# Attention scores in four row tiles, PSUM banks in rotating pairs, output products in column tiles

## The chip, the cores and the metric

One NeuronCore of one Trainium2 chip runs the whole program in one launch. The metric is the device time in microseconds, the median of several executions; lower is better. One further execution was taken with the hardware profiler.

## The reference

Two mixers work on 2048 tokens of 448 features and are blended by a gate for each token. Cut to what matters:

```python
def _A_ref(x, wq, wk, wv, wo):            # 16 heads of 28, one key and one value head
    q = (x @ wq).reshape(B, S, H, Dh).transpose(0, 2, 1, 3)
    k, v = x @ wk, x @ wv
    scores = einsum("bhqd,bkd->bhqk", q, k) * Dh ** -0.5
    o = einsum("bhqk,bkd->bhqd", softmax(scores), v)
    return o.transpose(0, 2, 1, 3).reshape(B, S, H * Dh) @ wo

def _B_ref(x, w1, w2, w3, w4):
    h = gelu(layernorm(x) @ w1)           # four groups of channels, shifted by +1, -1, +2, -2 tokens
    x1 = x + shifted(h) @ w2
    return x1 + gelu(layernorm(x1) @ w3) @ w4

g = sigmoid((x * gate_w).sum(-1))
out = g * _A_ref(...) + (1 - g) * _B_ref(...)
```

All of it is float32. Queries and keys are large here (`A_wq` and `A_wk` are scaled by over 40), so the scores need more than one rounded product: the kernel splits an operand into a rounded high part (type `F32R`) and the rest, and sums three products: high by high, high by low, low by high.

## The kernel before

The order of the instructions of every engine is the order in which the kernel writes them (`manual_schedule`). Waits come from a tracker of tiles: who writes a tile waits for the earlier readers of it. The kernel has three stages.

*Projections and token mixing.* `stage_q` makes queries, keys, values and gate sums from split products (`proj`: eleven matmuls of 512 columns into one PSUM bank); `q_out` copies them out with ScalarE (L297) and sends them to DRAM (`qd`). `stage_w1` and `stage_w2` do the first half of the second mixer. Products rotate over four banks (`mm1`: two of `mm_tile`, two of their own). `stage_kv` and `split_k` fetch the keys back and set them as three bands of 32 partitions (high, high, low) in `kS`.

*MLP.* For each of four blocks of 512 tokens and 14 chunks `f` of the hidden layer, `w3_part` makes a chunk with `proj` into one of two `mm_tile` banks, ScalarE takes two GELUs from the bank (L668, L669), VectorE makes the low part, and `w4_part` adds twelve products of 448 columns to four accumulators, two chunks behind. The last chunk of the last block is left for the next stage (`w4_job`).

*Attention.* A unit is four heads by 512 queries; there are 16 units of 16 key tiles (128 keys). For each key tile and head one matmul of 98 rows (three bands of 28 used rows and, in rows 96 and 97, the negated score maximum in two parts) gives the scores in a bank of its own (L901), and ScalarE takes the exponential into a tile `p` (L903). Seven banks rotate, and an eighth holds `pv`. Every few key tiles a visit (`VISITS`) does the products with the values (`pv_group`, L870): for each key tile four matmuls into the four column tiles of 32 of the array, side by side, in plain float32; they add up over the whole unit in `pv`. In between stand, at places written out by hand, estimates of the next unit's maxima (`max_part`, L210 and L211, over the first 32 keys), the products of the unit before with the output weights (`wo_job`, L812 to L816, three split products for each 128 tokens), the products left from the MLP (L841 to L845), and the splitting of the queries of a later unit (`q_begin`). At a unit's end VectorE copies `pv` out (L778); the sums of the exponentials go through memory (`sums_begin`, `recip`) and come back as factors for `norm` (L796).

After the last unit a tail transposes the last result, divides, does its output products and looks whether any sum overflowed; only then a slow second pass would run.

Of the kernel before, what the change touches and what calls it, by code (L numbers as in the profile page):

```python
# [31 lines left out]
PB = 22  # L32
# [9 lines left out]
def gated_mix_kernel(  # L42
# [25 lines left out]
    identR = keep.tile([P, P], F32R, name="identR")  # L68
    nc.vector.tensor_copy(identR, ident)
    x1 = keep.tile([P, NT, D], F32, name="x1")  # L70
    kS = keep.tile([P, S], F32R, name="kS")
# [14 lines left out]
    nc.gpsimd.memset(f32(kS)[96:128, :], 1.0)  # L86

    def mm_tile(name):
        return psA.tile([P, 512], F32, tag="mm", bufs=2, name=name)

    def misc_tile(name):
        return psA.tile([P, 512], F32, tag="misc", bufs=1, name=name)
# [86 lines left out]
    qs_of = [None, None]  # L179

    def q_load(u, raw):
        b, g = divmod(u, NG)
        qr_of[u] = raw
        nc.sync.dma_start(raw[0:4 * DH], qd[g, 0:4 * DH, 512 * b:512 * b + 512])

    def q_split(u, qh, ql):
        qr = qr_of.pop(u)[0:4 * DH]
        qh_of[u], ql_of[u] = qh[0:4 * DH], ql[0:4 * DH]
        nc.vector.tensor_copy(qh_of[u], qr)
        nc.vector.tensor_sub(ql_of[u], qr, f32(qh_of[u]))  # L190

    def q_rows(u):
        q_of[u] = qs_of[u % 2]
        for r, part in enumerate((qh_of[u], ql_of[u], qh_of[u])):
            nc.sync.dma_start(f32(q_of[u])[32 * r:32 * r + DH], f32(part))

    NU = NB * NG
    q_of = {}
    qr_of, qh_of, ql_of = {}, {}, {}
    mx_of = {}  # L200
    mc_of = {}

    def max_tile(name):
        return psA.tile([P, 512], F32, tag="mx", bufs=1, name=name)

    def max_part(u, t, tile_of):
        if t == 0:
            mx_of[u] = late.tile([P, 4, 4], F32, tag="mr", bufs=2, name=f"mr_{u}")
        ps = tile_of(f"m_{u}_{t}")[:, 0:4 * MK].rearrange("p (j k) -> p j k", j=4)
        nc.tensor.matmul(ps, qh_of[u][:, t * P:(t + 1) * P], khd[0:4 * DH], start=True, stop=True)  # L210
        nc.vector.reduce_max(mx_of[u][:, :, t], ps, axis=AX.X)  # L211

    def max_full(u, tile_of):
        mr = late.tile([P, 4, 4], F32, tag="mr", bufs=2, name=f"mf_{u}")
        for j in range(4):
            for t in range(4):
                mk = late.tile([P, NB], F32, tag="mk", bufs=2, name=f"mk_{u}_{j}_{t}")
                for kb in range(NB):
                    ps = tile_of(f"mf_{u}_{j}_{t}_{kb}")
                    nc.tensor.matmul(ps, q_of[u][0:96, j, t * P:(t + 1) * P], kS[0:96, kb * 512:kb * 512 + 512],  # L220
                                     start=True, stop=True)
                    nc.vector.reduce_max(mk[:, kb:kb + 1], ps, axis=AX.X)
                nc.vector.reduce_max(mr[:, j, t:t + 1], mk, axis=AX.X)
        mx_of[u] = mr

    def max_end(u):
# [7 lines left out]
        for p in range(4):  # L234
            nc.sync.dma_start(f32(qs_of[u % 2])[96:98, :, :].rearrange("k j (t p q) -> k p (j t) q", p=4, q=32)[:, p],
                              mrow[32 * p:32 * p + 32, :])
# [4 lines left out]
    with tc.tile_pool(name="s1b", bufs=1) as s1b, \  # L241
# [80 lines left out]
        kf_of = {}  # L322

        def stage_kv(b):
            cols = slice(512 * b, 512 * b + 512)
            kf = s1b.tile([96, 512], F32, tag="kf", bufs=2, name=f"kf_{b}")
            for r in range(3):
                for g in range(2):
                    nc.sync.dma_start(kf[32 * r + 16 * g:32 * r + 16 * g + 16, :], qd[g, 4 * DH:P, cols])
            for g in range(2):  # L330
                nc.sync.dma_start(vT[32 * b + 16 * g:32 * b + 16 * g + 16, :], qd[2 + g, 4 * DH:P, cols])
            kf_of[b] = kf

        def split_k(b):
            cols = slice(512 * b, 512 * b + 512)
            kf = kf_of[b]
            nc.gpsimd.tensor_copy(kS[0:96, cols], kf)
            nc.gpsimd.tensor_tensor(kS[64:96, cols], kf[64:96, :], f32(kS)[64:96, cols], ALU.subtract)
# [207 lines left out]
        split_k(0)  # L546
# [14 lines left out]
        split_k(1)  # L561
# [3 lines left out]
        split_k(2)  # L565
# [4 lines left out]
        khd = late.tile([P, 4, MK], F32R, name="khd")  # L570
        qh0 = late.tile([P, 512], F32R, tag="qh0", bufs=1, name="qh0")
        qs_of[0] = late.tile([P, 4, 512], F32R, name="qs0")
# [8 lines left out]
        def load_w34(i, pool):  # L581
            w3h.append(pool.tile([P, 4, 2 * P], F32R, name=f"w3h_{i}"))
            w3l.append(pool.tile([P, 4, 2 * P], F32R, name=f"w3l_{i}"))
            last = late if 2 * i + 2 == NF else pool
            w4h.append(last.tile([P, 2, D], F32R, name=f"w4h_{i}"))
            w4l.append(last.tile([P, 2, D], F32R, name=f"w4l_{i}"))
# [46 lines left out]
        split_k(3)  # L633
# [10 lines left out]
    with tc.tile_pool(name="s2", bufs=1, reuse_waits="tile") as s2, \  # L644
# [5 lines left out]
        fills = [lambda t=t: max_part(0, t, max_tile if t % 2 else misc_tile) for t in range(4)]  # L650
# [6 lines left out]
        def w3_part(b, f):  # L657
# [3 lines left out]
            if (b, f) == (NB - 1, NF - 1):  # L661
                gh = late.tile([P, 512], F32R, tag="qh0", bufs=1, name="gh_late")
                gl = late.tile([P, 512], F32R, name="gl_late")
            else:
                gh = s2.tile([P, 512], F32R, tag="gh", bufs=3, name=f"gh_{b}_{f}")
                gl = s2.tile([P, 512], F32R, tag="gl", bufs=3, name=f"gl_{b}_{f}")
            gf = s2.tile([P, 512], F32, tag="gf", bufs=2, name=f"gf_{b}_{f}")
# [14 lines left out]
        for b in range(NB):  # L682
            acc = [ps2.tile([P, 512], F32, tag="acc", bufs=4, name=f"acc_{b}_{t}") for t in range(4)]
            gs = {}
            for f in range(NF):
# [24 lines left out]
                if b == 1 and f == 1:  # L710
                    for z in (khd, qs_of[0][0:96]):
                        nc.gpsimd.memset(f32(z), 0.0)
                    for j in range(4):
                        nc.sync.dma_start(f32(khd)[j:4 * DH:4, j, :], f32(kS)[0:DH, 0:MK])
                    q_load(0, s2a.tile([P, 512], F32, tag="xn", bufs=1, name="qr_0"))
                if b == 1 and f == 5:
                    q_split(0, qh0, s2.tile([P, 512], F32R, tag="gl", bufs=3, name="ql_0"))
                    q_rows(0)
# [9 lines left out]
            if b == NB - 1:  # L728
                last_g = gs[NF - 1]
# [9 lines left out]
    with tc.tile_pool(name="s3", bufs=1, reuse_waits="tile") as s3, \  # L739
            tc.tile_pool(name="ps3", bufs=1, space=PSUM, reuse_waits="tile") as ps3:  # L740
        woh = s3.tile([P, 4, D], F32R, name="woh")
        wol = s3.tile([P, 4, D], F32R, name="wol")

        banks = [mm_tile("bank_0"), mm_tile("bank_1"), misc_tile("bank_2")]
        banks += [ps3.tile([P, 512], F32, name=f"bank_{i}") for i in range(3, 7)]

        def bank(name):
            ps = banks.pop(0)
            banks.append(ps)
            return ps  # L750

        qs_of[1] = s3.tile([P, 4, 512], F32R, name="qs1")
        nc.gpsimd.memset(f32(qs_of[1])[0:96], 0.0)
        def q_fetch(u):
            if u < NU:
                q_load(u, s3.tile([P, 512], F32, tag="qr", bufs=1, name=f"qr_{u}"))

        def q_begin(u):
            q_split(u, s3.tile([P, 512], F32R, tag="qh", bufs=2, name=f"qh_{u}"),
                    s3.tile([P, 512], F32R, tag="ql", bufs=1, name=f"ql_{u}"))  # L760
# [3 lines left out]
        q_rows(1)  # L764
# [11 lines left out]
        def sums_begin(u, pv):  # L776
            o = s3.tile([P, 512], F32, tag="o", bufs=2, name=f"o_{u}")
            nc.vector.tensor_copy(o, pv)  # L778
# [15 lines left out]
        def norm(u, o, rb):  # L794
            on = s3.tile([P, 512], F32, tag="onf", bufs=2, name=f"on_{u}")
            nc.vector.tensor_mul(on, o, rb)  # L796
            onh = s3.tile([P, 512], F32R, tag="onh", bufs=2, name=f"onh_{u}")
            onl = s3.tile([P, 512], F32R, tag="onl", bufs=2, name=f"onl_{u}")
            nc.gpsimd.tensor_copy(onh, on)  # L799
            nc.gpsimd.tensor_tensor(onl, on, f32(onh), ALU.subtract)  # L800
            on_of[u] = (onh, onl)
# [3 lines left out]
        def wo_job(u, t, end=None):  # L805
            b, g = divmod(u, NG)
            n = 4 * b + t
            tok = slice(t * P, (t + 1) * P)
            onh, onl = on_of[u]
            held = banks.pop(0)  # L810
            ps = held[:, 0:D]
            nc.tensor.matmul(ps, onh[:, tok], woh[:, g, :], start=True, stop=False)  # L812
            yield
            nc.tensor.matmul(ps, onh[:, tok], wol[:, g, :], start=False, stop=False)  # L814
            yield
            nc.tensor.matmul(ps, onl[:, tok], woh[:, g, :], start=False, stop=True)  # L816
            banks.append(held)
# [10 lines left out]
        woraw = s3.tile([P, 4, D], F32, name="woraw")  # L828
        nc.sync.dma_start(woraw, wo.rearrange("(g p) n -> p g n", p=P))
        nc.gpsimd.tensor_copy(woh, woraw)  # L830
        nc.gpsimd.tensor_tensor(wol, woraw, f32(woh), ALU.subtract)

        weigh_x1(NT - 4, NT)

        def w4_job(t):
            n = NT - 4 + t
            tok = slice(t * P, (t + 1) * P)
            gh, gl = last_g
            held = banks.pop(0)
            ps = held[:, 0:D]  # L840
            nc.tensor.matmul(ps, gh[:, tok], w4h[-1][:, 1, :], start=True, stop=False)  # L841
            yield
            nc.tensor.matmul(ps, gh[:, tok], w4l[-1][:, 1, :], start=False, stop=False)
# [249 lines left out]
```

## Time and profile before

| | |
|---|---|
| Median of 3 runs | 957.46 us (957.17 to 958.8) |
| Profiled execution, span from first to last instruction | 957.7 us; nothing is given of it beside the span |
| TensorE busy | 948.7 us, 99% |
| ScalarE busy | 648.2 us, 68% of the span; 94 us of each 100 in the attention stage |
| VectorE, GpSimd busy | 278.7 us, 115.9 us |
| First score product (L901), last value product (L870) | at 401.04 us; ends at 944.85 us |
| Granted TensorE clock | 0.998 on the mean |

PE is TensorE's matmuls, PEld its weight loads, DVE VectorE, ACT ScalarE, POOL GpSimd, SP SyncE. Times are in us, but the mean of one instruction in a group is in ns. A row of the timeline has the start, the length until the last of the merged instructions ends, the engine, the line, the operation, what it writes and reads, and how many; in brackets the idle time of the engine before it and what ended it. A row of a group has, after the bar, the time in which at least one of them ran, the mean of one, and the idle time before them. A row of the windows has the stretch, its length, the busy time of PE, PEld, DVE, ACT and POOL with the number of instructions, the granted clock, and the share and rate of the DMA engines. Matmuls overlap: a matmul's length holds the time that it needs to get through the array, so the distance from one start to the next is what a stream of them costs.

### The profile page before, as it was taken

How to read it: one execution, taken by the hardware profiler on the slowest of the kernel's cores; microseconds unless marked ns; L12 is line 12 of the kernel's file. 1: busy time of each engine (PE TensorE's matmuls, PEld its weight loads, DVE VectorE, ACT ScalarE, POOL GpSimd, SP SyncE). 2: the span in 40 equal slices, each digit the busy share in tenths (PEclk: the TensorE clock that was granted, in tenths of full speed). 3: DMA queues.
4: the chain of work that ended last, by engine and by line, in shares of the span. 5: the costliest groups of instructions: out<-in, count | busy, mean ns of one | idle time of the engine just before them, and what ended most of it. 6: DMA issues, size and time to landing. Idle time of an engine off the chain costs nothing.

```text
span 957.7 us, 13557 instructions
## 1 busy us (share of the span) xinstructions
PE 948.7 (99%) x5187; PEld 631.2 (66%) x5187; DVE 278.7 (29%) x573; ACT 648.2 (68%) x1266; POOL 115.9 (12%) x139
## 2 busy tenths in 40 slices
PE   9999999999999999999999999999999999999996
PEld 6788888888888888755555555455555555545544
DVE  4664364532423411221222112122121222212112
ACT  5532444332222222499999999999999999999994
POOL 3344300200001410040000000000000000000000
PEclk9999999999999999999999999999999999999999
DMA  9823552201300300111011021011111101210101
GB/s 312 274 70 76 144 165 83 80 14 29 83 1 1 83 1 10 28 54 48 21 42 42 22 79 52 27 26 51 52 51 40 51 13 40 80 51 9 35 13 42
DMA packets 45319, 57.33 MB, mean 60 GB/s; under 512 B 9856, under 2 KB 28096, under 8 KB 45248
## 3 DMA queue, kind: packets, MB, share of 16 engines
q1 hardware_dynamic: 42224, 50.93, 18.4%
q10 hardware_dynamic: 3024, 5.47, 1.5%
q8 instruction: 42, 0.69, 0.3%
q14 instruction: 29, 0.24, 0.1%
HBM read 32.19 MB, written 11.67 MB: 46 GB/s over the span
## 4 chain that ended last, share of the span: by engine, by line
PE 98%; DMA 1%; DVE 0%; ACT 0%; issue 0%; SPq 0%; ACTq 0%
PE bank L901 28%; PE pv L870 25%; PE acc L678 5%; PE acc L680 5%; PE acc L679 5%; PE g L134 4%; PE g L135 4%; PE g L136 4%; PE bank L816 1%; PE bank L814 1%; PE bank L812 1%; PE g L137 1%; PE g L138 1%; PE h L134 1%; PE h L135 1%; PE h L136 1%
## 5 line engine op out<-in xcount | busy, mean ns | idle before, releaser
L903 ACT ACTIVATE p<-bank 128x512 f32<-128x512 f32 x1024 | 511.4, 639 | 33.1 <-PE bank L901 30.7
L901 PE MATMUL bank<-qs,kS 98*128 98x512 f32 x1024 | 305.8, 410 | 0.0
L901 PEld LDWEIGHTS bank<-qs,kS 98*128 98x128 f32 x1024 | 184.1, 189 | 134.3 <-issue 93.1
L870 PE MATMUL pv<-p,vext 128*32 128x512 f32 x2048 | 243.1, 598 | 0.0
L668 ACT ACTIVATE gh<-g 128x512 fp32r<-128x512 f32 x55 | 32.9, 598 | 183.6 <-PE g L138 183.6
L870 PEld LDWEIGHTS pv<-p,vext 128*32 128x32 f32 x2048 | 58.9, 109 | 114.9 <-issue 108.0
L670 DVE TENSOR_TENSOR gl<-gf,gh 128x512 fp32r<-128x512 f32 x55 | 38.2, 695 | 163.6 <-ACT gf L669 159.3
L678 PE MATMUL acc<-w4h,gh 128*128 128x448 f32 x220 | 80.2, 365 | 0.0
L680 PE MATMUL acc<-w4h,gl 128*128 128x448 f32 x220 | 80.0, 364 | 0.0
L679 PE MATMUL acc<-w4l,gh 128*128 128x448 f32 x220 | 79.8, 363 | 0.0
L824 DVE SCALAR_TENSOR_TENSOR ot<-bank,gg,ot 128x448 f32<-128x448 f32 x44 | 30.0, 684 | 146.9 <-ACT p L903 95.1
L799 POOL CAST onh<-on 128x512 fp32r<-128x512 f32 x15 | 9.2, 611 | 471.8 <-DVE on L796 471.8
L134 PE MATMUL g<-ah,w3h 128*128 128x512 f32 x168 | 65.8, 392 | 0.0
L135 PE MATMUL g<-al,w3h 128*128 128x512 f32 x168 | 65.7, 391 | 0.0
L136 PE MATMUL g<-ah,w3l 128*128 128x512 f32 x168 | 65.7, 391 | 0.0
L211 DVE TENSOR_REDUCE mr<-bank 128x4 f32<-128x128 f32 x60 | 17.6, 293 | 108.5 <-PE bank L210 108.5
L678 PEld LDWEIGHTS acc<-w4h,gh 128*128 128x128 f32 x220 | 41.3, 188 | 4.2
L679 PEld LDWEIGHTS acc<-w4l,gh 128*128 128x128 f32 x220 | 41.3, 188 | 4.2
L680 PEld LDWEIGHTS acc<-w4h,gl 128*128 128x128 f32 x220 | 41.3, 188 | 3.1
L778 DVE COPY o<-pv 128x512 f32<-128x512 f32 x15 | 10.4, 692 | 99.4 <-PE pv L870 99.4
L136 PEld LDWEIGHTS g<-ah,w3l 128*128 128x128 f32 x168 | 31.5, 188 | 7.0
L135 PEld LDWEIGHTS g<-al,w3h 128*128 128x128 f32 x168 | 31.5, 188 | 5.7
(196 smaller groups left out, 965.5 us busy)
## 6 DMA issues: line engine op xcount, KB each, us to landing
qs<-qh SPq DMA_DIRECT2D x32, 224.0 KB
qd<-qf ACTq DMA_DIRECT2D x16, 256.0 KB
rb<-rd SPq DMA_DIRECT2D x15, 256.0 KB
x<-in_x_dram SPq DMA_DIRECT2D x4, 896.0 KB
xd<-xt SPq DMA_DIRECT2D x16, 224.0 KB
w34raw<-in_w_dram SPq DMA_DIRECT2D x7, 512.0 KB
qr<-qd SPq DMA_DIRECT2D x16, 224.0 KB
qs<-ql SPq DMA_DIRECT2D x16, 224.0 KB
```

Source lines behind the costliest of these rows:

```text
L134: nc.tensor.matmul(ps, wh[:, c, :], ah[:, c, :], start=(c == 0), stop=False)
L135: nc.tensor.matmul(ps, wh[:, c, :], al[:, c, :], start=False, stop=False)
L136: nc.tensor.matmul(ps, wl[:, c, :], ah[:, c, :], start=False, stop=False)
L668: nc.scalar.activation(gh, ps, AF.Gelu_apprx_tanh)
L670: nc.vector.tensor_sub(gl, gf, f32(gh))
L678: nc.tensor.matmul(ps, gh[:, tok], w4h[i][:, k, :], start=(f == 0), stop=False)
L679: nc.tensor.matmul(ps, gh[:, tok], w4l[i][:, k, :], start=False, stop=False)
L680: nc.tensor.matmul(ps, gl[:, tok], w4h[i][:, k, :], start=False, stop=(f == stop))
L824: nc.vector.scalar_tensor_tensor(ot_of[n], ps, gg[:, n:n + 1], before, op0=ALU.mult, op1=ALU.add)
L870: nc.tensor.matmul(pv[32 * j:32 * j + 32, :], vext[:, kt, :], ps[j], start=(kt == 0), stop=(kt == NT - 1), tile_position=(0, 32 * j))
L901: nc.tensor.matmul(ps, kS[0:98, kt * P:(kt + 1) * P], q_of[u][0:98, j, :], start=True, stop=True)
L903: nc.scalar.activation(p, ps, AF.Exp, scale=SCALE)
```

## The change

- Keys and queries stand in four bands of 32 partitions, one for each head: the keys four times (`kh` high, `kl` low), the queries one head a band (`qh`, `ql`), with the negated maxima in two more rows of a band. A key tile's scores are three rounds (high by high, high by low, low by high) of four matmuls, each 32 rows tall, in four row tiles of the array and into four PSUM banks.
- PSUM is four tiles of two banks. In the attention stage the pairs rotate: two for each key tile, and after every two key tiles a spare one, whose first half takes the value products of the two key tiles before, and whose second half takes a job. The earlier stages use two of these pairs: `mm_tile` gives the halves of `two_mm` in turn, `misc_tile` and `max_tile` the halves of `two_mx`.
- A step of the main loop is two key tiles. The first one's exponentials are two of 512 columns and one of 1024. Of the second one, VectorE copies the first pair to SBUF and ScalarE takes the exponential there in place; the second pair goes as before, 1024 at once. Thus five exponentials in a step instead of eight.
- The value products no longer add up over a unit in PSUM: each step's two key tiles are summed there, and VectorE adds them to `o` in SBUF (`values_end`).
- Output products, and those left from the MLP, are plain float32 in four column tiles of 32 tokens (`by_columns`); the splits of their operands are gone.
- The maxima of a unit are four matmuls into one bank with one reduction. `gf` has one buffer instead of two. `split_k` comes later, for all blocks together.

The core of the diff:

```diff
-PB = 22
+PB = 6
...
+    two_mm = psA.tile([P, 2, 512], F32, name="two_mm")
+    two_mx = psA.tile([P, 2, 512], F32, name="two_mx")
...
     def mm_tile(name):
-        return psA.tile([P, 512], F32, tag="mm", bufs=2, name=name)
+        mm_turn[0] += 1
+        return two_mm[:, (mm_turn[0] + 1) % 2]
...
+    def scores(u, kt, ps):
+        kh = kh_of[0]
+        keys = slice(kt * P, (kt + 1) * P)
+        for r, (k, q) in enumerate(((kh, qh_of[u]), (kh, ql_of[u]), (kl, qh_of[u]))):
+            for j in range(4):
+                h = slice(32 * j, 32 * j + 32)
+                nc.tensor.matmul(ps[j], k[h, keys], q[h, :], start=(r == 0), stop=(r == 2), tile_position=(32 * j, 0))
...
+        def values_end(u, pv):
+            if u not in o_of:
+                o_of[u] = s3.tile([P, 512], F32, tag="o", bufs=2, name=f"o_{u}")
+                nc.vector.tensor_copy(o_of[u], pv)
+            else:
+                nc.vector.tensor_add(o_of[u], o_of[u], pv)
...
+        def by_columns(ps, a, t, w):
+            for i in range(4):
+                c = t * P + 32 * i
+                nc.tensor.matmul(ps[32 * i:32 * i + 32, :], a[:, c:c + 32], w, start=True, stop=True,
+                                 tile_position=(0, 32 * i))
...
+        for c in range(NU * NT // 2 + 1):
+            u, i = divmod(c, NT // 2)
+            k = 2 * c
+            if u < NU:
+                ps, p = score_tiles(u, 2 * i, "p")
+                exps(p, slice(0, 1), ps[0][:, 0:1])
+                exps(p, slice(1, 2), ps[0][:, 1:2])
+                exps(p, high, ps[1])
+                p_of[k] = p
+                ps, p = score_tiles(u, 2 * i + 1, "p")
+                nc.vector.tensor_copy(p[:, low], ps[0])
+                exps(p, high, ps[1])
+                exps(p, low)
+                p_of[k + 1] = p
+            spare = pair()
+            if c:
+                v = divmod(c - 1, NT // 2)[0]
+                pv = spare[:, 0]
+                values(k - 2, pv, True, False)
+                values(k - 1, pv, False, True)
+                if (v, i) != (NU - 1, 0):
+                    values_end(v, pv)
...
+            if i == 3 and u + 1 < NU:
+                max_part(u + 1, range(4), spare[:, 1])
+                max_end(u + 1)
+            elif i > 3 and jobs:
+                jobs.pop(0)(spare[:, 1])
```

Here `score_tiles` takes two pairs and calls `scores`, `exps` is one ScalarE instruction over the named heads, and `values` is the four matmuls of one key tile with the values, as before.

More of the change, by code (lines that the diff above doesn't have):

```diff
@@ L794, in norm, with wo_job @@
         def norm(u, o, rb):
[L795 to L801, printed above, removed]
+            on_of[u] = s3.tile([P, 512], F32, tag="on", bufs=2, name=f"on_{u}")
+            nc.vector.tensor_mul(on_of[u], o, rb)
+        def by_columns(ps, a, t, w):
[3 more added lines that the diff above has]
+                                 tile_position=(0, 32 * i))
         ot_of = {}
-        def wo_job(u, t, end=None):
+        def wo_job(u, t, bank, end=None):
             b, g = divmod(u, NG)
             n = 4 * b + t
[L808 to L817, printed above, removed]
+            ps = bank[:, 0:D]
+            by_columns(ps, on_of[u], t, wof[:, g, :])
             before = x1[:, n, :] if g == 0 else ot_of[n]
@@ L826, in wo_job, with w4_job @@
                 nc.sync.dma_start(out[0, n * P:(n + 1) * P, :], ot_of[n])
[L828 to L831, printed above, removed]
         weigh_x1(NT - 4, NT)
-        def w4_job(t):
+        def w4_job(t, bank):
             n = NT - 4 + t
[L837 to L843, printed above, removed]
-            yield
-            nc.tensor.matmul(ps, gl[:, tok], w4h[-1][:, 1, :], start=False, stop=True)
-            banks.append(held)
-            nc.vector.scalar_tensor_tensor(x1[:, n, :], ps, gi[:, n:n + 1], x1[:, n, :], op0=ALU.mult, op1=ALU.add)
@@ L864, in pv_group, with exps, score_tiles, values @@
+        p_of = {}
+        def exps(p, heads, source=None):
+            nc.scalar.activation(p[:, heads], p[:, heads] if source is None else source, AF.Exp, scale=SCALE)
+        def score_tiles(u, kt, name):
+            ps = [pair(), pair()]
+            scores(u, kt, [ps[j // 2][:, j % 2] for j in range(4)])
+            return ps, s3.tile([P, 4, 512], F32, tag="p", bufs=PB, name=f"{name}_{u}_{kt}")
+        def values(k, pv, first, last):
             u, kt = divmod(k, NT)
-            if kt == 0:
-                pv_of[u] = max_tile(f"pv_{u}")
@@ L924, in gated_mix_kernel @@
-        assert not sums and not norms
-        u = NU - 1
-        pv = pv_of.pop(u)
-        o = s3.tile([P, 512], F32, tag="o", bufs=2, name=f"o_{u}")
-        onh = s3.tile([P, 512], F32R, tag="onh", bufs=2, name=f"onh_{u}")
-        onl = s3.tile([P, 512], F32R, tag="onl", bufs=2, name=f"onl_{u}")
-        on_of[u] = (onh, onl)
+                nc.tensor.matmul(pv[32 * j:32 * j + 32, :], vext[:, kt, :], p[:, j],
+                                 start=first, stop=last, tile_position=(0, 32 * j))
@@ L932, in gated_mix_kernel, with bank @@
+        assert not sums and not norms and not jobs
+        u = NU - 1
+        banks = [q[:, h] for q in pairs for h in range(2)]
+        def bank(name):
+            ps = banks.pop(0)
+            banks.append(ps)
+            return ps
+        part = o_of.pop(u)
+        o = s3.tile([P, 512], F32, tag="o", bufs=2, name=f"oo_{u}")
+        on = s3.tile([P, 512], F32, tag="on", bufs=2, name=f"on_{u}")
+        on_of[u] = on
         toks = [slice(t * P, (t + 1) * P) for t in range(4)]
@@ L969, in tail_wo @@
         def tail_wo(t):
[L970 to L971 removed]
+            wo_job(u, t, bank(f"wo_{t}"), end)
         def keep_warm(n):
```

291 lines of the change are left out of this document (117 added, 174 removed).

## The prediction

> **What bounds the kernel now.** First the head of the page and its chain of work:
>
> ```profile
> span 957.7 us, 13557 instructions
> PE 948.7 (99%) x5187; PEld 631.2 (66%) x5187; DVE 278.7 (29%) x573; ACT 648.2 (68%) x1266; POOL 115.9 (12%) x139
> PE 98%; DMA 1%; DVE 0%; ACT 0%; issue 0%; SPq 0%; ACTq 0%
> PE bank L901 28%; PE pv L870 25%; PE acc L678 5%; PE acc L680 5%; PE acc L679 5%; PE g L134 4%; PE g L135 4%; PE g L136 4%; PE bank L816 1%; PE bank L814 1%; PE bank L812 1%; PE g L137 1%; PE g L138 1%; PE h L134 1%; PE h L135 1%; PE h L136 1%
> ```
>
> TensorE is the chain, and the scores (L901) with the products with the values (L870) are over half of it. The span stands 0.2 us above the median of the runs, so both serve. Next the attention stage by windows, and its groups:
>
> ```profile
> 500.00:600.00 100.00, 100.00 (x612) 53.39 (x608) 21.27 (x51) 94.05 (x189) 5.66 (x6) 1.00 0.16 47
> L903 ACT ACTIVATE p<-bank 128x512 f32<-128x512 f32 x1024 | 511.4, 639 | 33.1 <-PE bank L901 30.7
> ```
>
> ScalarE is busy 94 us in 100 and TensorE all of them: two engines near their limits, covered by seven PSUM banks in rotation. The period of a unit (four heads, 512 queries) is read off the copies of `pv`, 14 units apart, in the timeline:
>
> ```profile
> 436.85 0.69 DVE L778 COPY o<-pv 128x512 f32<-128x512 f32 x1 [2.55 <-PE pv L870]
> 912.39 0.69 DVE L778 COPY o<-pv 128x512 f32<-128x512 f32 x1 [6.92 <-PE pv L870]
> 602.61 2.13 PE L901 MATMUL bank<-qs,kS 98*128 98x512 f32 x8
> 604.67 1.92 PE L870 MATMUL pv<-p,vext 128*32 128x512 f32 x16
> 606.52 0.72 PE L901 MATMUL bank<-qs,kS 98*128 98x512 f32 x2
> 457.03 2.78 PE L870 MATMUL pv<-p,vext 128*32 128x512 f32 x24
> 940.58 1.20 PE L901 MATMUL bank<-qs,kS 98*128 98x512 f32 x4
> 941.62 0.37 PE L812 MATMUL bank<-woh,onh 128*128 128x448 f32 x1
> 941.83 0.37 PE L814 MATMUL bank<-wol,onh 128*128 128x448 f32 x1
> ```
>
> 475.54/14 = 33.97 us. Eight scores take 2.13 and four 1.20, so a score slot is 0.2325, and one alone 2.13 - 7x0.2325 = 0.50. A group of four value products side by side (half of a key tile) is (2.78-1.92)/2 = 0.43, so a key tile is 0.86. From the start of a visit of two key tiles to the next score is 1.85, of which 1.72 streams: 0.13 is the change of array shape, and 0.50-0.2325 = 0.27 more stands at the first score. Sum of a unit: 64x0.2325 + 16x0.86 + 12 output products x 0.21 + 7 visits x 0.40 = 14.9 + 13.8 + 2.5 + 2.8 = 34.0. TensorE's own streaming is the period; waits play no part.
>
> **The change, as work.** Four heads score at once in three rounds, so twelve matmuls take three slots instead of four, if a round costs one slot. No row shows row tiles. Below: one slot, 0.2325, for 512 columns have to stream. Above: the loads of four weight tiles one after another.
>
> ```profile
> 432.56 0.30 PEld L901 LDWEIGHTS bank<-qs,kS 98*128 98x128 f32 x2 [0.84 <-issue]
> 463.99 0.16 PEld L870 LDWEIGHTS pv<-p,vext 128*32 128x32 f32 x8 [0.36 <-issue]
> L870 PEld LDWEIGHTS pv<-p,vext 128*32 128x32 f32 x2048 | 58.9, 109 | 114.9 <-issue 108.0
> 460.34 5.99 ACT L903 ACTIVATE p<-bank 128x512 f32<-128x512 f32 x12 [0.85 <-PE bank L901]
> 467.30 5.04 ACT L903 ACTIVATE p<-bank 128x512 f32<-128x512 f32 x10 [0.98 <-PE bank L901]
> L125 ACT CAST ahk<-xkv 128x1024 fp32r<-128x1024 f32 x4 | 4.0, 1048 | 1.0 <-DMA xkv<-in_xT_dram 0.6 <-ACT qf L297 0.5
> ```
>
> Two 128-column loads into the whole array take 0.30 together; if the first lasts 0.19, the second starts 0.11 after it, so four are up to 0.44 a round. But eight loads into four column tiles take 0.16, where one alone lasts 0.109: tiles load side by side there. Row tiles are nearest to those, and I take 0.2325. ScalarE: exps of 512 start (5.99-5.04)/2 = 0.475 apart and last 0.64, so each overlaps the next by 0.165. A 1024 cast lasts 1.05; less the same overlap a 1024-wide exp costs about 0.90 (two of 512, 0.95, are the upper bound). Two key tiles now need two of 512 and three of 1024: 0.95 + 2.70 = 3.65 against 8x0.475 = 3.80. Both engines would fit in 3.65x8 = 29.2 us a unit. What decides is the order.
>
> **The loop that the order makes.** A step is two key tiles. Its PSUM pairs are A,B (first tile), C,D (second), then A again as the spare pair for the value products of the step before; B is A of the next step. TensorE's written order is S1 (into A,B), S2 (into C,D), V (into A), the job (into A's other half), next S1. V may start only when ScalarE has read both banks of A, that is after exps e1 and e2 of this step; e1 needs S1; and the next S1 stands behind V. So e1, e2, V, S1, e1 is one closed loop with nothing of it overlapped: exactly what seven single banks avoided. The other three exps hide in it. The hand-overs:
>
> ```profile
> 434.81 1.92 PE L870 MATMUL pv<-p,vext 128*32 128x512 f32 x16
> 941.18 2.07 ACT L903 ACTIVATE p<-bank 128x512 f32<-128x512 f32 x4 [0.36 <-PE bank L901]
> 946.73 0.29 DVE L946 TENSOR_TENSOR on<-bank,rr 128x128 f32<-128x128 f32 x1
> 947.08 0.33 PE L951 MATMUL bank<-ident,on 128*128 128x128 f32 x1
> 437.22 0.23 PE L210 MATMUL bank<-khd,qh 112*128 112x128 f32 x1
> 437.28 1.61 PE L901 MATMUL bank<-qs,kS 98*128 98x512 f32 x6
> ```
>
> TensorE to ScalarE: the lone score ends at 940.58+0.50 = 941.08, its exp starts 941.18: 0.10. To VectorE: 434.81+1.92 = 436.73, the copy at 436.85: 0.12. Back to TensorE: 947.02 to 947.08: 0.06, which I also take after ScalarE.
>
> A step without a job: e1 to e2 0.475; e2 lasts 0.64 (mean 639 of L903); 0.06; V 1.85 until the next score may enter; S1 = 0.50 + 2x0.2325 = 0.97; 0.10. Sum 4.10.
>
> A step with a job: in the built order the first matmul of each job, and the key maxima's too, waits for VectorE. Nothing in its bank asks for that; but the pair is one tile, and `values_end` still reads its first half. So V runs to its end 1.92 (not 1.85), 0.12, the addition 0.69 (as the copy L778), 0.06, then the job. An output product in column tiles is four passes of 448 columns: 2x0.43x448/512 = 0.75, plus 0.13 for the change = 0.88 (bounds: three slots of 0.21 below, a full key tile with both changes, 1.26, above). Sum 0.475+0.64+0.06+1.92+0.12+0.69+0.06+0.88+0.97+0.10 = 5.92. The step with the maxima: four matmuls of 0.06 (437.22 to 437.28), a load of 0.11 and a further change of 0.2 make 0.55 in place of 0.88: 5.59.
>
> Eight steps: three at 4.10, four at 5.92, one at 5.59 = 41.6 us, against 33.97. Sixteen units: **+122 us**.
>
> **The head.** The pairs also serve the stages before. `mm_tile` is now half of one tile, so a product into the second half waits until the readers of the first are done:
>
> ```profile
> 198.08 0.39 PE L138 MATMUL g<-ah,w3l 128*128 128x512 f32 x1
> 198.31 0.39 PE L134 MATMUL g<-ah,w3h 128*128 128x512 f32 x1
> 199.00 0.59 ACT L669 ACTIVATE gf<-g 128x512 f32<-128x512 f32 x1
> 25.78 0.75 PE L134 MATMUL q<-ahk,wqh 128*128 128x512 f32 x1
> 27.80 0.59 ACT L297 COPY qf<-q 128x512 f32<-128x512 f32 x1 [1.23 <-DMA qd<-qf]
> ```
>
> In the MLP the product at 198.31 would wait for 199.00+0.59, then 0.06 and a load of 0.11: 199.76, a loss of 1.45. From f = 2 on twelve products of `w4_part` (12x0.21 = 2.5 us) cover it; f = 1 and f = 2 of each of four blocks are bare: 8x1.45 = 11.6. In the projections seven of 26 products meet the other half: the first at 25.78 would wait until 28.39+0.17, 2.8; six more some 1.0 (the product's end 0.39, hand-over, copy 0.59, 0.17, less a slot): 9 in all. The first unit's maxima share a pair too: 1. Head **+21 us**.
>
> Tail: TensorE's last values start after the last job instead of beside it, 1.92, and the output products are 0.88 against 0.6 each, four of them: **+3**, between 0 and 7.
>
> At nothing, with what hides it: VectorE gets a 1024 copy (twice 0.69 at most) and an addition of 0.69 a step, 2.1 of 4.1, and where it is late only e5 is late, which nothing reads before the next V. GpSimd loses the splits of `on`.
>
> ```profile
> 446.85 2.69 SPq L235 DMA_DIRECT2D qs<-mrow x4
> 439.57 0.25 DVE L787 RECIPROCAL rr<-rt 128x16 f32<-128x16 f32 x1
> 446.71 0.65 DVE L796 TENSOR_TENSOR on<-o,rb 128x512 f32<-128x512 f32 x1
> ```
>
> SyncE issues eight maxima rows, four query loads and three transfers of sums a unit (eleven in all before): 15x0.67 = 10 of 41 us, and the maxima are read four steps later. The reciprocals' way through memory has two steps, 8.2 us, and now takes 446.71-439.57 = 7.1 at most; uncovered, it would cost a microsecond a unit.
>
> Sum: 957.7 + 122 + 21 + 3 = **1104 us**.
>
> **The rivals.** *ScalarE binds (faster).* If V did not hold S1 back, the step would be 3.65: 16x(29.2-33.97) = -76, with the head 903 us, without it 882. For it: TensorE has work for only some 3.6 of a step. Against: it decides from the point where e1, e2, V, S1 close in under 3.65 with the jobs in, and V and S1 alone are 2.82. Chance 0.04.
>
> *Weight loads of row tiles don't overlap.* Then the change doesn't do what it says: a round is 0.44, twelve matmuls cost more than before, and S1, the part in the loop, grows by 3x0.21 in 128 steps: +80, 1184. For it: 128-column loads stand 0.11 apart. Against: column tiles load side by side. Chance 0.08. *Half of that*, a round of 0.34: 1145, chance 0.14. The Trainium skill, "TensorE: Matmul & The Clock Gate", Part 3 (Packing small matmuls), gives 3.07 times for four row tiles with 512 columns instead of 4; no row here shows it, and by it the sum would be 1131, an estimate.
>
> *The jobs' wait is met already.* If the wait were for an older VectorE instruction, each of five steps a unit loses 0.94: -75, 1029. Chance 0.05.
>
> **The numbers.** The forecast's own case holds 0.68: with hand-overs at their lowest (0.04 each) 1085, with the job at 1.26 and the tail at 7 1132. The likeliest is 1104. The range 1078 to 1150 takes in that case and the half-overlapped loads, 0.82 together, and leaves out both ends. About 0.2% is what a measurement of this kernel tells from none (957.17 to 958.8). Faster 0.04, same 0.01, slower 0.95.
>
> **What would show it.** Right: the chain of work alternates TensorE, ScalarE and, in job steps, VectorE; ScalarE is idle before each e1 for TensorE, about 0.4 us without a job and 2 with one; the unit is 41 to 42 us; the first score starts near 422. Wrong: ScalarE over 95% busy in the stage; rounds of twelve over 1.2 us; no TensorE wait for `values_end`; gaps that bring the granted clock, now 1.00, down.

## The result and the profile after

The changed kernel takes 1109.74 us (median of 4 runs, 1107.35 to 1111.78) against 957.32 us (956.79 to 958.8): 1.1591 times as long, 95% interval 1.1573 to 1.161. The forecast was 1104 us in 1078 to 1150. The profiled execution took 1111.78 us with a span of 1110.0, 1.8 us outside the span; readings of the trace are set against the span. First the head of the page:

```profile
span 1110.0 us, 18322 instructions
...
PE 963.3 (87%) x7575; PEld 568.6 (51%) x7575; DVE 501.8 (45%) x766; ACT 629.7 (57%) x877; POOL 80.8 (7%) x111
```

And of the windows the one that was shown of before:

```profile
500.00:600.00 100.00, 81.91 (x856) 33.52 (x856) 50.89 (x69) 72.71 (x96) 0.00 (x0) 1.00 0.05 14
```

TensorE was busy 100 us of 100 and ScalarE 94; now it is 82 and 73. No engine is full: each waits for another. The page's chain of waits is empty for this kernel ("DVE 0%; issue 0%"), so the prediction's sign of an alternating chain can't be read, and the loop has to be taken from the waits and the timeline. The waits (engine and line, what it waited for, us in all, times, longest):

```profile
ACT p L848 <- PE pair L208: 73.8, 64, 2.3
...
PEld pair L817 <- DVE o L791: 57.0, 32, 1.8
...
PEld pair L859 <- ACT p L848: 48.8, 64, 1.1
...
PEld two_mm L140 <- ACT gf L678: 12.8, 8, 1.6
...
PEld two_mm L140 <- ACT qf L310: 5.6, 3, 3.4
...
PEld two_mm L140 <- DVE hf L447: 5.0, 4, 1.3
```

The first three, each with rows of the same kind for the other pairs, are the loop and the job's wait: ScalarE's exponentials wait for scores, output products (L817) for VectorE's addition (L791), values (L859) for exponentials. The last three are the stages ahead: products that wait for the readers of the other half of their pair. Then one step without a job and one with, on the timeline:

```profile
643.02 1.09 ACT L848 ACTIVATE p<-two_mx 128x512 f32<-128x512 f32 x2 [0.19 <-PE pair L208]
...
644.16 1.92 PE L859 MATMUL two_mx<-p,vext 128*32 128x512 f32 x16 [0.30 <-ACT p L848]
...
646.01 0.51 PE L208 MATMUL pair<-qh,kh 32*128 32x512 f32 x4
...
646.35 0.41 PE L208 MATMUL pair<-ql,kh 32*128 32x512 f32 x4
...
646.58 0.41 PE L208 MATMUL pair<-qh,kl 32*128 32x512 f32 x4
...
647.07 2.00 ACT L848 ACTIVATE p<-pair 128x512 f32<-128x512 f32 x3 [0.20 <-PE pair L208]
...
657.85 1.92 PE L859 MATMUL two_mm<-p,vext 128*32 128x512 f32 x16 [0.38 <-ACT p L848]
...
659.91 0.69 DVE L791 TENSOR_TENSOR o<-o,two_mm 128x512 f32<-128x512 f32 x1 [1.27 <-PE two_mm L859]
...
660.65 0.96 PE L817 MATMUL two_mm<-wof,on 128*32 128x448 f32 x8 [0.88 <-DVE o L791]
...
661.54 0.50 PE L208 MATMUL two_mx<-qh,kh 32*128 32x512 f32 x2
...
662.61 1.08 ACT L848 ACTIVATE p<-two_mx 128x512 f32<-128x512 f32 x2 [2.04 <-PE pair L208]
...
663.75 1.92 PE L859 MATMUL two_mx<-p,vext 128*32 128x512 f32 x16 [0.36 <-ACT p L848]
```

From e1 at 643.02 through V at 644.16 and S1 at 646.01 to the next e1 at 647.07 is 4.05. With a job, V (657.85), the addition, the job, S1 and e1 and V again (663.75) close in 5.90. Every member waits for the one ahead of it. Last, the line that copies a unit's first values (least, middle and greatest ns, first and last start), and the first score and the last values on the timeline:

```profile
L789 DVE COPY o<-two_mx x16: 691/692/693, 439.4 to 1060.0; 128x512 f32<-128x512 f32 x16
```

```profile
424.03 0.50 PE L208 MATMUL two_mm<-qh,kh 32*128 32x512 f32 x2
...
1091.30 1.90 PE L859 MATMUL two_mm<-p,vext 128*32 128x512 f32 x16
```

A unit is (1060.0-439.4)/15 = 41.4 us. The head ends at 424.03 (before 401.04: +23.0), the stage lasts 669.2 (before 543.8: +125.4), and 16.8 us follow the last value product (before 12.9: +3.9): together the 152.3 by which the spans differ.

### The profile page after: what moved, and what is told of

Read it like the earlier page. It is cut to its first block, busy times and chain, and to the rows that moved or that the text cites. A ratio compares the mean times of both kernels' runs of the same rounds, so it can differ in the third digit from the quotient of the medians.

```text
span 1110.0 us, 18322 instructions
## 1 busy us (share of the span) xinstructions
PE 963.3 (87%) x7575; PEld 568.6 (51%) x7575; DVE 501.8 (45%) x766; ACT 629.7 (57%) x877; POOL 80.8 (7%) x111
## 5 line engine op out<-in xcount | busy, mean ns | idle before, releaser
L848 ACT ACTIVATE p<-pair 128x1024 f32<-128x1024 f32 (+1 forms) x256 | 198.7, 817 | 73.6 <-PE pair L208 38.2
L859 PE MATMUL pair<-p,vext 128*32 128x512 f32 x1024 | 123.1, 598 | 20.9 <-ACT p L848 20.9
L848 ACT ACTIVATE p<-p 128x1024 f32<-128x1024 f32 x128 | 138.1, 1079 | 3.5 <-DVE p L877 3.5
L848 ACT ACTIVATE p<-two_mm 128x1024 f32<-128x1024 f32 (+1 forms) x128 | 101.2, 817 | 57.5 <-PE two_mx L208 55.8
L848 ACT ACTIVATE p<-two_mx 128x1024 f32<-128x1024 f32 (+1 forms) x128 | 101.2, 817 | 35.8 <-PE pair L208 35.6
L877 DVE COPY p<-pair 128x1024 f32<-128x1024 f32 x64 | 78.4, 1225 | 51.0 <-PE pair L208 49.8
L208 PE MATMUL pair<-qh,kh 32*128 32x512 f32 x512 | 95.3, 472 | 3.9 <-DVE p L877 3.9
L208 PE MATMUL pair<-ql,kh 32*128 32x512 f32 x512 | 82.0, 393 | 0.0
L208 PE MATMUL pair<-qh,kl 32*128 32x512 f32 x512 | 81.8, 391 | 0.0
L791 DVE TENSOR_TENSOR o<-o,pair 128x512 f32<-128x512 f32 x64 | 44.0, 688 | 79.8 <-PE pair L859 79.8
L140 PE MATMUL two_mm<-ah,w3h 128*128 128x512 f32 x168 | 66.8, 397 | 9.4 <-ACT gf L678 9.4
L859 PE MATMUL two_mx<-p,vext 128*32 128x512 f32 x512 | 63.3, 613 | 10.2 <-ACT p L848 10.2
L859 PE MATMUL two_mm<-p,vext 128*32 128x512 f32 x512 | 61.5, 598 | 11.3 <-ACT p L848 11.3
L859 PEld LDWEIGHTS pair<-p,vext 128*32 128x32 f32 x1024 | 26.7, 109 | 87.1 <-ACT p L848 48.8
```

Of the source, the lines that this page charges most:

```text
L140: nc.tensor.matmul(ps, wh[:, c, :], ah[:, c, :], start=(c == 0), stop=False)
L208: nc.tensor.matmul(ps[j], k[h, keys], q[h, :], start=(r == 0), stop=(r == 2), tile_position=(32 * j, 0))
L791: nc.vector.tensor_add(o_of[u], o_of[u], pv)
L848: nc.scalar.activation(p[:, heads], p[:, heads] if source is None else source, AF.Exp, scale=SCALE)
L859: nc.tensor.matmul(pv[32 * j:32 * j + 32, :], vext[:, kt, :], p[:, j], start=first, stop=last, tile_position=(0, 32 * j))
L877: nc.vector.tensor_copy(p[:, low], ps[0])
```

## The experiments

Each was measured beside the kernel before (957.67 to 958.27 us in these groups). My theory was the prediction's: losses that come from who waits for whom, not from work.

**The job ahead of the addition.** In steps with a job or the maxima:

```diff
-                if (v, i) != (NU - 1, 0):
+                if i < 3 and (v, i) != (NU - 1, 0):
                     values_end(v, pv)
...
                 jobs.pop(0)(spare[:, 1])
+            if i >= 3:
+                values_end(v, pv)
```

> The changed kernel, but in the steps with a job or the maxima (i >= 3) `values_end` is issued behind the job instead of ahead of it. My theory (TensorE waits there for VectorE's addition, which reads the other half of the same pair tile, and that wait lies in the loop e1, e2, V, S1): each of five steps a unit loses 0.12+0.69+0.06 and 0.07 = 0.94 us, so 5.9 becomes 5.0 and 5.6 becomes 4.7; the unit 41.3 becomes 36.6 to 37.5; 16 units -60 to -75: 1035 to 1050 us. TensorE's waits before L817 for VectorE's o (57 us in all) nearly go. Rival, the jobs are dear by themselves on TensorE (their own 0.9 and the changes of shape): the wait is only moved to the next score, and the time stays 1105 to 1112. Rival, the head and tail carry the loss: 1110 too.

Measured 1054.06 us, 1.1004 times before (1.0986 to 1.1022): -55.7. The timeline of this kernel, a job step and then the score that follows a maxima step:

```profile
642.30 1.92 PE L859 MATMUL two_mx<-p,vext 128*32 128x512 f32 x16
...
644.04 0.94 PE L817 MATMUL two_mx<-wof,on 128*32 128x448 f32 x8
...
645.73 0.68 DVE L791 TENSOR_TENSOR o<-o,two_mx 128x512 f32<-128x512 f32 x1
...
646.46 0.50 PE L208 MATMUL two_mx<-qh,kh 32*128 32x512 f32 x2 [0.35 <-DVE o L791]
...
647.36 1.92 PE L859 MATMUL pair<-p,vext 128*32 128x512 f32 x16
...
635.66 0.64 DVE L791 TENSOR_TENSOR o<-o,pair 128x512 f32<-128x512 f32 x1
...
636.36 0.50 PE L208 MATMUL pair<-qh,kh 32*128 32x512 f32 x2 [0.96 <-DVE o L791]
```

The job follows the values without a wait, and the job step is 5.06 (V at 642.30 and 647.36) instead of 5.89: the theory holds for the jobs. The time misses the range of 1035 to 1050 all the same: the addition is now late for the second half of S2 (0.35), and in the maxima step, where it queues behind the maxima's VectorE work, 0.96; that step only fell from 5.59 to 5.50. The stall was moved on in part. (The 57 us of the expectation are the rows of `pair` alone; with `two_mm` and `two_mx` the jobs waited 114 us.)

**Single banks ahead of the attention.** The pairs are made only in the attention stage:

```diff
+    psH = head_banks.enter_context(tc.tile_pool(name="psH", bufs=1, space=PSUM))
...
     def mm_tile(name):
-        mm_turn[0] += 1
-        return two_mm[:, (mm_turn[0] + 1) % 2]
+        return psH.tile([P, 512], F32, tag="mm", bufs=2, name=name)
```

> The changed kernel, but the stages ahead of the attention take single-bank PSUM tiles out of a pool of their own, which is closed before the attention; the attention's four pairs stay as they are. My theory (halves of one pair tile make a product wait for the readers of the other half, 23 us by the first score's start, 424.0 against 401.0): first score at 401 to 403, the attention stage unchanged at 669 us, 1086 to 1090 us in all. Rival, the head is later because of what else changed there (the DMAs of keys and queries, the splits of keys on GpSimd, the product left for the jobs): the first score stays at 420 to 424 and the time at 1106 to 1111.

Measured 1085.64 us, 1.1329 times before (1.131 to 1.1348): -24.1. The stage's first score in this kernel:

```profile
400.00 0.50 PE L206 MATMUL pair<-qh,kh 32*128 32x512 f32 x4
```

401.04 before, 424.03 changed, 400.00 here, and the stage stays at 667.7. The head's loss was the halves of pairs, with what their waits do to the clock (below), and nothing else.

**One round less, in the loop and outside it.** The third round of the first key tile (then of the second) of each step is left out:

```diff
+            scores(u, kt, [...], 2 if kt % 2 == 0 else 3)    # the other run: kt % 2 == 1
```

> Leaves out part of the scores: the third round of split products (four matmuls, 0.2325 us by the first kernel's slot) of the first key tile of each step, 128 rounds in all. It is in the loop S1, e1, e2, V. My theory: each step is shorter by one round, 128x0.2325 = 30 us: 1078 to 1083. Rival, ScalarE sets the step: 1106 to 1111. Rival, TensorE's sum of work sets it: 1080, as my theory; the run that tells these two apart is the one with the second tile's round left out.

> Leaves out the third round of split products of the second key tile of each step instead (again 128 rounds). That tile's scores run while ScalarE does e1 and e2, outside the loop. My theory: the time stays within 4 us of the changed kernel, 1106 to 1112. Rival, TensorE's sum of work sets the step: -30, 1078 to 1083. Rival, ScalarE sets it: no change, as my theory; but then leaving out the first tile's round brings nothing either.

Measured 1084.94 us without the first tile's round (1.1324 times before, 1.1305 to 1.1343) and 1109.84 without the second's (1.1581, 1.1561 to 1.16): -24.8 and +0.1 for the same work taken away. Value products of two steps without a job, first of the one, then of the other:

```profile
600.03 1.92 PE L859 MATMUL pair<-p,vext 128*32 128x512 f32 x16
...
603.85 1.92 PE L859 MATMUL pair<-p,vext 128*32 128x512 f32 x16
```

```profile
602.00 1.92 PE L859 MATMUL two_mx<-p,vext 128*32 128x512 f32 x16 [0.53 <-ACT p L848]
...
606.06 1.92 PE L859 MATMUL pair<-p,vext 128*32 128x512 f32 x16 [0.51 <-ACT p L848]
```

A step is 3.82 in the first kernel and still 4.06 in the second, where the wait of V has grown from 0.30 to 0.53: the round of 0.23 was turned into idle time. This is the run that shows the loop and rules out TensorE's sum of work and ScalarE. The first kernel lies 2 us above the range that I gave. Its trace has one unit that is 2.3 us longer than the others, half of what is missing to -29.4 (128 rounds of 0.23):

```profile
647.18 0.69 DVE L812 TENSOR_TENSOR on<-o,rb 128x512 f32<-128x512 f32 x1 [1.13 <-DMA rb<-rd]
...
648.53 0.79 PE L208 MATMUL pair<-qh,kh 32*128 32x512 f32 x2 [0.87 <-DVE mr L217]
```

There the factors for `norm` come late from memory, the maxima's reduction (L217) stands behind `norm` on VectorE, and TensorE waits 0.87 for it. In this wait the granted clock falls to half (0.57 on the mean of 648 to 652 us), so that these scores last 0.79 instead of 0.50.

**Both first edits together.** 

> Both earlier edits in the changed kernel: `values_end` behind the job, and single-bank tiles ahead of the attention; the attention keeps its four pairs. My theory (the two losses lie one behind the other, in different stages): the sum of what each brought alone, -55.7 and -24.1 from 1109.7: 1029 to 1031 us, steps without a job still 4.06. Rival, both shorten the same wait: 1050 or above.

Measured 1028.98 us, 1.0742 times before (1.0723 to 1.0761): -80.8, where the two alone make -79.8. The losses lie one behind the other.

**Eight single banks.** The same order, with `pair` taking two tiles out of a ring of eight, one exponential and one copy for each head:

```diff
-        pairs = [two_mm, two_mx] + [ps3.tile([P, 2, 512], F32, name=f"pair_{i}") for i in range(2, 4)]
+        ring = [mm_tile("bank_0"), mm_tile("bank_1"), misc_tile("bank_2"), max_tile("bank_3")]
+        ring += [ps3.tile([P, 512], F32, name=f"bank_{i}") for i in range(4, 8)]
```

> The changed kernel with its scores in row tiles, its visits, jobs and VectorE's copies in the same order, but with eight single-bank PSUM tiles in rotation everywhere instead of four pairs; ScalarE's direct exps are then 512 wide (six a step) and VectorE copies two heads in two instructions. The values then wait for e1 alone, the job for no addition, and the next tile's scores for single banks. My theory (the loop e1, e2, V, S1 and the wait for the addition are all of the loss): a step without a job is set by ScalarE, 6x0.475+0.90 = 3.75, a job step by TensorE, 6x0.23+0.27+1.85+0.88 = 4.4, the maxima step about 5; unit 33.8, beside 33.97 before; head back to 401, tail +4: 955 to 970 us. Rival, the change is dear even without the pairs (eight visits, the jobs in float32 column tiles, the copies): 1025 or above, as with the two edits alone.

Measured 971.01 us, 1.0134 times before (1.0116 to 1.0152): 138.7 of the 152 us are gone, and with the new work all still in. A microsecond above what I expected: the unit is 34.17 and not 33.8. The window, and the timeline around a job:

```profile
500.00:600.00 100.00, 98.25 (x1044) 41.69 (x1036) 62.99 (x110) 92.60 (x167) 0.00 (x0) 1.00 0.09 26
```

```profile
642.95 0.94 PE L813 MATMUL bank<-wof,on 128*32 128x448 f32 x8
643.27 0.69 DVE L787 TENSOR_TENSOR o<-o,bank 128x512 f32<-128x512 f32 x1 [0.75 <-PE bank L855]
...
644.87 3.05 ACT L844 ACTIVATE p<-bank 128x512 f32<-128x512 f32 x6 [0.46 <-PE bank L203]
...
648.70 3.10 ACT L844 ACTIVATE p<-bank 128x512 f32<-128x512 f32 x6
```

TensorE is busy 98 us of 100 again. The job (642.95) starts ahead of the addition (643.27). After a job step ScalarE idles 0.46 for scores, after a step without one not at all.

**The job ahead of the values, on single banks.**

```diff
...
+                if i == 2 and u + 1 < NU:
+                    max_part(u + 1, range(4), one())
+                elif i in (4, 5, 6, 7) and jobs:
+                    jobs.pop(0)(one())
             if c:
-                pv = spare[0]
+                pv = one()
                 values(k - 2, pv, True, False)
...
+            if i == 2 and u + 1 < NU:
+                max_end(u + 1)
```

> The single-bank kernel of the run before, with the order inside a step changed: the job (or the maxima, now at i = 2) is issued ahead of the values, each takes one bank of the ring as it needs it (nine banks in steps without a job, ten with one), and the end of the maxima and `norm` are queued on VectorE behind `values_end`; the next queries are split at i = 1. My theory (what is left over the sum of TensorE's work are next scores that wait for VectorE's addition and for the maxima's reduction): 3 steps of 3.75, 4 of 4.42, 1 of 4.1 to 4.4 make a unit of 33.0 to 33.4; with the head at 400 and a tail of 16: 940 to 952 us, below both kernels (957.5). Rival, VectorE's place in the order is covered already: as the run before, 955 to 970. Rival, ScalarE binds every step: 8x3.75 and jobs hidden, 30 a unit, 900.

Measured 957.77 us, 0.9993 times before (0.9984 to 1.0002): the kernel before again, to within the measurement. The order brought 13.2 us; the unit fell to 33.4, the upper end of what I expected, but the total missed the range. The stage is 541.8 us and sixteen units only 534; I had overlooked something at its start (below).

**Half jobs.**

```diff
+        cut = (slice(0, D), slice(0, D // 2), slice(D // 2, D))
...
-            by_columns(ps, on_of[u], t, wof[:, g, :])
+            by_columns(ps, on_of[u], t, wof[:, g, c])
```

> The kernel of the run before (single banks, job ahead of the values), with each output product cut into two halves of 224 columns and one half issued in every step but that of the maxima (two at i = 5), instead of a whole one in four steps of eight; the other half of VectorE's sum with it. In the run before, steps without a job were 3.66 to 3.76 us with ScalarE never idle, and steps with one 4.43 with ScalarE idle 0.33. My theory (the two engines bind in turn, so an even load saves what each idles): TensorE 3.46+0.375+0.14 = 3.98 in six steps, 4.1 with the maxima, 4.5 with two halves: a unit of 32.5 instead of 33.4, 941 to 947 us. Rival, each extra change of shape costs what the balance brings: 955 to 960. Rival, TensorE is full in all steps already: four more changes of 0.14 a unit, 960 to 968.

Measured 955.27 us, 0.9972 times before (0.9959 to 0.9986): above the 941 to 947 that I expected and in the range of the rival that each change of shape costs what the balance brings. Steps are 4.06 and not 3.98:

```profile
664.17 1.90 PE L862 MATMUL bank<-p,vext 128*32 128x512 f32 x16
...
666.20 0.69 DVE L790 TENSOR_TENSOR o<-o,bank 128x512 f32<-128x512 f32 x1 [0.83 <-ACT p L851]
...
666.94 0.18 PEld L203 LDWEIGHTS bank<-qh,kh 32*128 32x128 f32 x1 [0.17 <-DVE o L790]
...
667.06 3.04 ACT L851 ACTIVATE p<-bank 128x512 f32<-128x512 f32 x6
...
667.83 0.58 PE L816 MATMUL bank<-wof,on 128*32 128x224 f32 x8
...
668.24 1.90 PE L862 MATMUL bank<-p,vext 128*32 128x512 f32 x16
```

A smaller loop of the same kind is left, and it runs through VectorE. A step needs ten banks of eight, so the fourth head of the second key tile takes the bank that V has just left: V (664.17) ends, the addition (666.20) reads its bank, that head's scores start after it (666.94) and end a slot behind the other three, then come the job (667.83) and the next V (668.24). ScalarE stands close behind: e1 (667.06), which frees the job's bank, lasts 0.60 and is over 0.17 before the job starts. This is read from the rows; no run takes work out of this loop, and TensorE's busy share is 100 of 100 there, so the rivals are not ruled out by experiment.

**The start of the stage.** What was overlooked is seen in the changed kernel's own timeline and windows:

```profile
430.44 0.43 DVE L199 CAST qh<-qr 128x512 fp32r<-128x512 f32 x1 [5.67 <-DMA qr<-qd]
...
431.51 1.22 DVE L877 COPY p<-pair 128x1024 f32<-128x1024 f32 x1
...
432.78 0.79 PE L208 MATMUL pair<-qh,kh 32*128 32x512 f32 x2 [3.85 <-DVE p L877]
```

```profile
432.00:436.00 4.00, 3.22 (x26) 2.03 (x30) 1.32 (x2) 3.00 (x5) 0.00 (x0) 0.50 0.20 61
```

The queries of unit 1 come in four transfers instead of one (the eight of the expectation are those of two units), VectorE waits 5.67 us to split them, the first copy of scores stands behind that in its queue, and TensorE waits 3.85 for the copy. Two kernels move that split behind the second step:

```diff
-        q_begin(1)
-        q_fetch(2)
...
+            if c == 1:
+                q_begin(1)
+                q_fetch(2)
```

> The changed kernel, but the split of unit 1's queries (`q_begin(1)`, with the fetch of unit 2's) is issued after the second step of the attention instead of ahead of the first. In the changed kernel that split stands ahead of VectorE's first copy of scores and waits 5.67 us for its eight query loads; the copy starts at 431.51 where its scores were ready at about 425.9, and the second step's first exponential starts at 434.06, 7.7 us after the first step's. My theory (the step before the copy then costs 4 us): that exponential starts at about 430.3, -3.8: 1105 to 1107 us. Rival, the start of ScalarE's table and the query loads set it: 1109 to 1111.

> The kernel with half jobs, with the same edit (`q_begin(1)` after the second step, unit 2's queries split at i = 5). My theory: the same 3.8 us: 950 to 953 us, 0.5 to 0.8% below the kernel before. Rival, as above: 955.

Measured 1103.19 us for the changed kernel with this edit (1.1515 times before, 1.1495 to 1.1535) and 950.49 for the half jobs with it (0.9918, 0.99 to 0.9935). The stage alone went from 669.2 to 664.5 and from 539.4 to 534.6, 4.7 and 4.8 in the two traces, a little over the 3.8 expected. The 4.8 hold two things: with half jobs the granted clock was 0.50 from 407 to 411 us without the edit, and with it the clock stays at 1.00. The rest of the first difference lies ahead of the stage, where the edit does nothing and the clock did (see the head, below). The last of these kernels is 0.8% faster than the kernel before. What the row tiles have of that isn't shown, since no run takes them without the rest of the change.

## Why the prediction was right

*TensorE bounds before, and neither engine after.* Right: 82 and 73 of 100.

*A round costs one slot.* Right: rounds start at 646.35 and 646.58, 0.23 apart, and a round less in the loop shortens a step by 0.23. That ends both rivals in which weight loads stand in the way. The Trainium skill, "TensorE: Matmul & The Clock Gate", Part 3 (Packing small matmuls), has 3.07 times for four row tiles with 512 columns; by these rows it is four heads in the 0.23 of one, 4 times.

*The loop.* Right in each kind of step: 4.06 for 4.10, 5.89 for 5.92, 5.59 for 5.59; the unit 41.4 for 41.6. Its parts too: V starts 1.14 after e1 (1.18 forecast), S1 1.85 after V (1.85), the next e1 1.06 after S1 (1.07). ScalarE's wait before e1 is 2.04 with a job, as said, and 0.2 without one, where I said 0.4. That the pairs, not the work, make it, is shown by single banks (-58 beyond the first two edits); the addition's part by the job moved ahead (-55.7). That the wait is the tile's and not the bank's follows from the single-bank kernel, in which nothing but the tiles and the widths of ScalarE's and VectorE's instructions is different and the job's wait for the addition is gone.

*The head.* 21 forecast, 23.0 by the trace, 24.1 by the experiment. The count was exact: 8 waits for GELUs and 7 in the stages ahead of the MLP. Of the 13.0 us that are added from the MLP to the first score I had 12.6 with the first maxima. Ahead of that the first product of the MLP starts at 136.75 instead of 126.75, 10.0 later where I had 9, but these 10.0 are not waits alone. The same wait of a product for the copies of the other half, in the changed kernel and in the one with the late split, which does not differ there:

```profile
26.99 0.79 PE L140 MATMUL two_mm<-ahk,wqh 128*128 128x512 f32 x1 [2.69 <-ACT qf L310]
```

```profile
26.62 0.50 PE L140 MATMUL two_mm<-ahk,wqh 128*128 128x512 f32 x1 [2.73 <-ACT qf L310]
```

In the first trace the granted clock is 0.50 from 28 to 32 us, in the second 1.00. There the MLP starts at 133.42, and at 134.07 with the job moved ahead, where the clock stayed up as well. So at full clock these stages are some 7 us later than before (8 to 10 later than in the kernels with single banks, where the MLP starts at 124.2 to 125.5), near the 9 of the forecast; a clock at half, which the sum doesn't have, brought some 3 more in the execution that was profiled. That 10.0 and 9 agree so well is in part luck.

*The tail.* 3 forecast, 3.9 measured.

*The step that failed* is the one that put VectorE and SyncE at nothing: "where it is late only e5 is late, which nothing reads before the next V". Inside a unit that held. At the first step it did not: the bank that the late copy reads is wanted by the next scores, and the query loads, which I had priced against a whole unit, have no unit to hide in there. It cost 4.7 us, nearly what the median exceeds the forecast by (5.7). The stage is 669.2 and not 16x41.4 = 662; sixteen units alone would have made the sum a little too large. What is left of the 7 us beyond the 4.7 is likely the clock: with the late split, too, TensorE works at half speed for some 6 us at the start of the stage (last section), which by my estimate costs half of that, and no run takes it apart.

*The granted clock* stayed at 1.00 in the changed kernel's loop, as forecast, but neither at the first step nor, in the profiled execution, in the projections (last section).

*Rivals.* "ScalarE binds" is out by the first tile's round, whose absence leaves ScalarE's work as it is and shortens the step, and "the jobs' wait is met already" by the job moved ahead. As far as the rows show, ScalarE bound nothing until the single banks, and there only in steps without a job.

## What to carry to other kernels

When buffers rotate, write down for one round which instruction frees which buffer, and follow it once around: the longest closed path is the period, however busy or idle the engines are, and work taken away outside it buys nothing (+0.1 us here, against -24.8 for the same work inside). Two banks in one tile are one lock for whoever tracks tiles; that, and not the new arithmetic, cost 139 of 152 us. Count the first round by itself, since transfers that hide in a steady loop have nothing to hide in there.

## What the runs showed of the hardware that was not expected

Four row tiles load their weights at the same moment, in the time of one; this row of the changed kernel has four loads in 0.19, where I had bounds up to 0.44 for a round:

```profile
646.01 0.19 PEld L208 LDWEIGHTS pair<-qh,kh 32*128 32x128 f32 x4 [0.84 <-ACT p L848]
```

A pause of TensorE can halve its clock, which then stays at half for longer than the pause, but the length of the pause alone doesn't decide it. In the changed kernel with the late split (timeline, then a window):

```profile
425.07 0.79 PE L208 MATMUL two_mx<-qh,kh 32*128 32x512 f32 x2 [2.63 <-ACT p L846]
...
427.95 3.53 PE L857 MATMUL two_mx<-p,vext 128*32 128x512 f32 x16
...
431.41 0.50 PE L208 MATMUL pair<-qh,kh 32*128 32x512 f32 x4
```

```profile
424.00:428.00 4.00, 2.93 (x28) 1.91 (x31) 0.00 (x0) 4.00 (x7) 2.92 (x3) 0.55 0.44 146
```

The value products last 3.53 instead of 1.92, and from 425.07 to about 431.4, 6.3 us, all is at half speed. The like pauses of 2.69 and 2.73 us in the projections (above) halved it in one trace and not in the other, and the run without the first tile's third round had it halved in the middle of the loop, with no pause over 0.9 us near by. The Trainium skill, "TensorE: Matmul & The Clock Gate", Part 1, lets the clock fall after an idle window of about 3.4 us and rise after one that is busy; here shorter pauses were at times enough. By the granted clock in narrow windows, the stretches at half speed lasted 3.4 us in that run's loop, 6.8 with the late split and 10.2 at the first step of the changed kernel: one, two and three times 3.4. In the changed kernel's own loop, where TensorE pauses for 1.22 us at most, the clock stayed at 1.00.
